# Second chunk of a mixture of experts: third token block first, then two blocks by seven products, gate weights in memory of their own

## The chip, the cores and the metric

The kernel runs on one core of a Trainium2 chip. The metric is the device time of one execution in microseconds (us), lower is better. The core's engines are named as in the profile: PE (TensorE, matmuls; PEld is its weight load), DVE (VectorE), ACT (ScalarE), POOL (GpSimd) and SP, whose queue issues the DMAs. Each engine works through its own instructions in order.

## The reference, cut to what matters

```python
x = attention(q, k, v, n_sink, window)          # (1536, 512) after the heads are put side by side
logits = x @ w_gate                             # 8 experts
P = np.exp(logits - logits.max())
for _ in range(8):                              # rows, then columns
    P /= P.sum(1, keepdims=True) + 1e-09
    P /= P.sum(0, keepdims=True) + 1e-09
    P *= N / E
for e in range(8):                              # w1: 512 x 1024, w2: 1024 x 512
    out += P[:, e:e+1] * (np.maximum(x @ w1[e], 0) @ w2[e])
y = (np.maximum(out @ w_in, 0) ** 2) @ w_out    # 512 -> 2048 -> 512
```

## The kernel before, in words

The work after the attention goes in chunks `c` of 512 hidden columns: 16 of the experts (two per expert) and 4 of the last layer. A chunk has a first layer (x times its part of w1), an evacuation (relu) into `h`, and a second layer (`h` times its part of w2, added to `acc`). The 1536 tokens are three blocks `t` of 512. Every operand of a matmul is kept as a rounded high part and a low part (`xh` and `xl`, `w2h` and `w2l`, `hh` and `hl`), and one product is three matmuls: low times high, high times high, high times low.

A **split** makes the two parts (`pair_split`): ACT copies the raw values into the high part, which rounds them, and POOL subtracts that from the raw values into the low part. Weights come by DMA into one of three buffers of the pool `raw` and are split from there: `units` for w1, `part_w2` for the four pieces of w2. `load_list` is the order of the loads; `next_loads` issues one when an earlier one has been used.

Two forms of the first layer exist. `plain(c, t, f)` computes one 128-column group `f` of one block directly, in 12 matmuls of 512 columns. `fast(c, half, q)` computes, for half of the hidden columns, two blocks together (`q` = 0: blocks 0 and 1) or the two halves of the third block (`q` = 1) by seven products of 6 matmuls each where the direct way takes eight (a scheme of Strassen's kind). It needs four sums of parts of x, T1 to T4, made once by `sums(q)` on DVE, each then split by ACT and POOL, and four sums of parts of w1, made by `unit_sums` on POOL (lines with raw<-raw) and split by `units` with `which` = 3 (tiles s0, s1). T1 is written over the part of `xh` and `xl` that only the direct way needs. The products of a half are p1, p6, p5, p2, p7, p3, p4 in this order, each followed by its evacuation step e1, e6, ... : p2 adds onto the sum in PSUM that p1 began, after ACT has copied it out in e1; likewise p4 after e7, and p3 after e5.

Chunk 0's first layer and most of its second are woven into the attention (`phase_a`; `fill` holds what is left over, finished at the start of `phase_b`). Chunk 1 is all `plain`: block 1, then 0, then 2, while `sums` makes the T tiles between its groups. Chunks 2 to 15 use `fast` for all three blocks. The order of the instructions is written out by hand: within a chunk, `seq` is the list of PE groups, and `put(k, step)` hangs a step behind group `k`. The steps of a group are issued to their engines' queues in the order in which they were put. `GATE_AT` says behind which groups of `phase_b` the next step of `gate` is issued: three steps with 8 matmuls each on the gate's weights `wgz`, one that takes the maximum, and ten that make P. Each of the last eight is a matmul with `ones` of a column sum `cs`, then six small DVE instructions that end in the next `cs`.

The second layer, `second(c, t)`, has four groups of 12 matmuls, each over the four pieces f of `h` and w2 in this order:

```python
for f in (0, 1, 3, 2):
    for x, w in ((hh, wh), (hh, wl), (hl, wh)):
```

## Time and profile before

| | |
|---|---|
| median of 3 runs | 1379.75 us (1378.94 to 1380.15) |
| profiled execution | 1379.64 us |
| its span in the profile | 1377.8 us |
| PE busy | 1363.2 us, 99% of the span |
| POOL busy | 501.3 us, 36% |

The time of an execution includes about 1.8 us around the span that the profile shows. Matmuls overlap in the profile: one of 512 columns lasts 0.39 us there, while the next begins 0.23 us after it, so stages are read from starts and not from the sum of durations. A row of a timeline gives the start and duration in us, then engine, line, operation, out<-in, shape, how many such instructions were merged, and in brackets the idle time before and what ended it.

### The profile page before, as it was taken

What the parts mean: (1) busy time and instruction counts of PE and PEld (TensorE: products, weight loads), DVE (VectorE), ACT (ScalarE), POOL (GpSimd) and SP (SyncE); (2) the same over time, 40 slices, a digit from 0 to 9 for tenths busy, and PEclk for the clock granted to TensorE, in tenths of its full rate; (3) what the DMA queues carried; (4) which work ended last, traced back from release to release, by engine and by line L of the source; (5) the groups of instructions that cost most, each with busy time, mean ns of one, the idle gap of its engine ahead of it and who ended that gap; (6) DMA issues with size and microseconds to landing.
All of it is one profiled execution on the core that took longest, in us unless ns stands there. A gap on an engine that the chain in (4) does not pass through costs nothing.

```text
span 1377.8 us, 18905 instructions
## 1 busy us (share of the span) xinstructions
PE 1363.2 (99%) x7105; PEld 1141.7 (83%) x7105; DVE 955.4 (69%) x1884; ACT 453.1 (33%) x1007; POOL 501.3 (36%) x442
## 2 busy tenths in 40 slices
PE   8999999999999999999999999999999999999998
PEld 5677888888888888888888888888888888888887
DVE  8777369887777777777777768765454568866564
ACT  6776322322232222222232222222232243433331
POOL 4322136524343434424343434423343036543210
PEclk9999999999999999999999999999999999999999
DMA  5222200132313232232313232230102010111101
GB/s 203 81 90 73 78 31 31 62 94 73 124 54 109 79 96 85 92 107 67 118 54 122 70 95 82 92 107 32 61 32 77 16 62 16 62 55 54 46 24 72
DMA packets 61147, 102.53 MB, mean 74 GB/s; under 512 B 3957, under 2 KB 43253, under 8 KB 60789
## 3 DMA queue, kind: packets, MB, share of 16 engines
q1 hardware_dynamic: 61040, 101.22, 23.2%
q8 instruction: 58, 0.95, 0.3%
q14 instruction: 45, 0.36, 0.1%
q10 hardware_dynamic: 4, 0.00, 0.0%
HBM read 89.67 MB, written 11.53 MB: 73 GB/s over the span
## 4 chain that ended last, share of the span: by engine, by line
PE 79%; DVE 1%; ACT 0%; issue 0%; DVEq 0%; ACTq 0%
PE mm L913 42%; PE mm L762 36%; PE mm L930 0%; ACT tx L733 0%; DVE acc L653 0%; DVE tx L734 0%; ACT hh L745 0%; DVE tx L822 0%; DVE hl L746 0%; DVE acc L649 0%; DVE mm L734 0%; DVE raw L578 0%; ACT tx L836 0%; DVE tu L822 0%; DVE raw L565 0%
## 5 line engine op out<-in xcount | busy, mean ns | idle before, releaser
L913 PE MATMUL mm<-w2h,hh 128*128 128x512 f32 (+1 forms) x916 | 357.0, 390 | 0.0
L913 PE MATMUL mm<-w2l,hh 128*128 128x512 f32 (+1 forms) x916 | 355.9, 388 | 0.0
L913 PE MATMUL mm<-w2h,hl 128*128 128x512 f32 (+1 forms) x916 | 355.6, 388 | 0.0
L482 POOL TENSOR_TENSOR w2l<-raw,w2h 128x512 fp32r<-128x512 f32 x76 | 118.5, 1559 | 365.7 <-ACT w2h L481 363.7
L653 DVE SCALAR_TENSOR_TENSOR acc<-mm,P,acc 128x512 f32<-128x512 f32 x168 | 125.7, 748 | 135.6 <-PE mm L913 134.4
L913 PEld LDWEIGHTS mm<-w2h,hl 128*128 128x128 f32 x916 | 172.0, 188 | 35.8
L913 PEld LDWEIGHTS mm<-w2h,hh 128*128 128x128 f32 x916 | 172.1, 188 | 34.6
L913 PEld LDWEIGHTS mm<-w2l,hh 128*128 128x128 f32 x916 | 172.1, 188 | 34.3
L525 POOL TENSOR_TENSOR raw<-raw 128x256 f32<-128x256 f32 x136 | 125.1, 923 | 7.9
L482 POOL TENSOR_TENSOR s0l<-raw,s0h 128x512 fp32r<-128x512 f32 (+1 forms) x36 | 45.5, 1264 | 198.6 <-ACT s0h L481 198.6
L730 ACT ACTIVATE hh<-tx 128x512 fp32r<-128x512 f32 (+1 forms) x112 | 58.8, 525 | 130.0 <-DVE tx L822 129.5
L822 DVE TENSOR_TENSOR tx<-mm,tu 128x512 f32<-128x512 f32 (+1 forms) x136 | 75.6, 556 | 20.9 <-PE mm L762 16.6
L822 DVE TENSOR_TENSOR tx<-mm,tx 128x512 f32<-128x512 f32 (+1 forms) x68 | 37.9, 557 | 57.8 <-PE mm L762 56.5
L740 DVE SCALAR_TENSOR_TENSOR hl<-tx,hh 128x512 fp32r<-128x512 f32 (+1 forms) x112 | 70.1, 626 | 9.7 <-ACT hh L730 9.6
L836 ACT ACTIVATE tx<-mm 128x512 f32<-128x512 f32 x34 | 20.3, 598 | 154.9 <-PE mm L762 153.0
L646 DVE TENSOR_TENSOR acc<-mm,acc 128x512 f32<-128x512 f32 (+1 forms) x49 | 33.2, 677 | 48.2 <-PE mm L913 47.9
L730 ACT ACTIVATE hh<-mm 128x512 fp32r<-128x512 f32 (+1 forms) x68 | 34.0, 501 | 99.2 <-PE mm L762 99.2
L836 ACT ACTIVATE txs<-mm 128x256 f32<-128x256 f32 x34 | 13.0, 381 | 151.3 <-PE mm L762 151.3
L482 POOL TENSOR_TENSOR a0l<-raw,a0h 128x512 fp32r<-128x512 f32 (+1 forms) x38 | 43.0, 1148 | 51.5 <-ACT a0h L481 47.5
L762 PE MATMUL mm<-xl,a1h 128*128 128x512 f32 (+1 forms) x172 | 60.3, 350 | 0.2 <-ACT tx L836 0.2
L762 PE MATMUL mm<-xl,a0h 128*128 128x512 f32 (+1 forms) x172 | 59.8, 348 | 0.0
L762 PE MATMUL mm<-xh,a0h 128*128 128x512 f32 (+1 forms) x172 | 59.8, 347 | 0.0
(262 smaller groups left out, 3149.5 us busy)
## 6 DMA issues: line engine op xcount, KB each, us to landing
raw<-w SPq DMA_DIRECT2D x110, 512.0 KB, 3.7
raw<-win SPq DMA_DIRECT2D x16, 512.0 KB, 4.0
w<-m SPq DMA_DIRECT2D x32, 256.0 KB, 4.6
raw<-wout SPq DMA_DIRECT2D x16, 512.0 KB, 4.0
raw<-qkv SPq DMA_DIRECT2D x8, 624.0 KB, 5.0
raw<-qkv SPq DMA_DIRECT2D x7, 464.0 KB, 3.9
out<-acc SPq DMA_DIRECT2D x11, 256.0 KB, 2.0
wraw<-w SPq DMA_DIRECT2D x2, 1024.0 KB, 6.7
```

Of the source, the lines that this page charges most:

```text
L482: self.nc.gpsimd.tensor_tensor(out=lo, in0=src, in1=hi.bitcast(F32), op=ALU.subtract)
L525: self.nc.gpsimd.tensor_tensor(out=o, in0=x, in1=y, op=op)
L646: nc.vector.tensor_tensor(out=a, in0=ps, in1=a, op=ALU.add)
L653: nc.vector.scalar_tensor_tensor(out=a, in0=ps, scalar=self.P[:, ti, e : e + 1], in1=a, op0=ALU.mult, op1=ALU.add)
L730: nc.scalar.activation(out=hh, in_=src, func=AF.Relu)
L740: nc.vector.scalar_tensor_tensor(out=hl, in0=src, scalar=0.0, in1=hh.bitcast(F32), op0=ALU.max, op1=ALU.subtract,)
L762: self.nc.tensor.matmul(out=ps, lhsT=w[:, kc], rhs=x[:, kc], start=start and k == 0, stop=(k == n - 1), skip_group_check=True,)
L822: nc.vector.tensor_tensor(out=v[name], in0=v[a], in1=v[b], op=ALU.add)
L836: nc.scalar.activation(out=v["s"], in_=v["a"], func=AF.Copy)
L913: self.nc.tensor.matmul(out=ps[:, d], lhsT=x[:, f, s], rhs=w[:, f, d], start=(n == 0), stop=(n == 11),)
```

## The change

The two arrays for the gate get memory of their own (`gw0`), their load and split are issued in the attention at steps 22 and 25, and `ones` is made at the start. The first four steps of the gate are issued behind the groups of `fill`, the others at the places in the second list of `GATE_AT`. Chunk 1 takes block 2 first, by `plain`, with its second layer right behind, then blocks 0 and 1 by `fast` (`mixed`), then their second layers. For this the loads (1, 3, 0) and (1, 3, 1) are added, `unit_sums` and `units` with `which` = 3 for chunk 1, and a form of `sums` that makes T1 first. The four pieces of w2 are put behind groups 0, 0, 1 and 1 in place of 0, 1, 2 and 3.

```diff
--- before.py
+++ after.py
@@ -38,7 +38,10 @@
 NC = NC1 + NC2
 CONV = 3
 CONV_AT = (0, 1, 2, 3, 8, 9, 10, 11, 12, 13, 14, 15)
-GATE_AT = (0, 1, 2, 3, 5, 7, 9, 11, 13, 16, 19, 22, 25, 30)
+GATE_AT = (
+    (0, 1, 2, 3, 5, 7, 9, 11, 13, 16, 19, 22, 25, 30),
+    (12, 14, 16, 18, 20, 22, 25, 28, 31, 36),
+)
 W2_AT = (2, 5, 8, 11)
 NB = 512
 BIG = 1e30
@@ -99,6 +102,8 @@
         )
         self.ident = c.tile([128, 128], F32, name="ident")
         make_identity(nc, self.ident)
+        self.ones = c.tile([128, 128], F32, name="ones")
+        nc.gpsimd.memset(self.ones, 1.0)
         a = self.att
         self.junk = a.tile([128, 1], F32, name="junk")
         self.m0 = a.tile([128, 128], F32, name="m0")
@@ -436,6 +441,9 @@
     def load_list(self, c0):
 
         loads, k = [(c0, which, half) for which in range(2) for half in range(2)], 0
+        if c0:
+            loads[2:2] = [(c0, 3, 0)]
+            loads.append((c0, 3, 1))
         for c in range(c0, NC):
             wide = [(j, 2, 0) for j in range(k, min(k + CONV, 8 * NC2)) if c >= 2]
             k += len(wide)
@@ -668,14 +676,15 @@
         o = 2 * NB * q + w * t
         return tuple(x[:, k : k + 2, o : o + w] for x in (self.xh, self.xl))
 
-    def sums(self, q):
-
-        nc = self.nc
-        T = [
+    def T_tiles(self, q):
+        self.T[q] = [
             self.tp.tile([128, 3, 2, NB >> q], F32R, tag=f"T{q}{t}", name=f"T{q}{t}")
             for t in "hl"
         ]
-        self.T[q] = T
+
+    def sums(self, q, t1_first=False):
+
+        nc = self.nc
 
         def tt(o, a, b, op):
             if isinstance(o, str):
@@ -690,6 +699,30 @@
             hi, lo = self.operand(name, q)
             self.pair_split(hi[:, kc], lo[:, kc], x)
 
+        if t1_first:
+            for kc in range(2):
+                x = tt("x0", f32("B12", 0, kc), f32("B11", 0, kc), ALU.subtract)
+                tt(x, x, f32("B12", 1, kc), ALU.add)
+                tt(x, x, f32("B11", 1, kc), ALU.subtract)
+                put("T1", kc, x)
+            yield
+            self.T_tiles(q)
+            for kc in range(2):
+                t2 = tt("u", f32("B22", 0, kc), f32("B12", 0, kc), ALU.subtract)
+                tt(t2, t2, f32("B22", 1, kc), ALU.add)
+                tt(t2, t2, f32("B12", 1, kc), ALU.subtract)
+                put("T2", kc, t2)
+                yield
+                t4 = tt("x2", f32("B21", 0, kc), t2, ALU.subtract)
+                tt(t4, t4, f32("B21", 1, kc), ALU.add)
+                put("T4", kc, t4)
+                yield
+                t3 = tt("x0", t2, f32("B11", 0, kc), ALU.subtract)
+                tt(t3, t3, f32("B11", 1, kc), ALU.subtract)
+                put("T3", kc, t3)
+                yield
+            return
+        self.T_tiles(q)
         for kc in range(2):
             x = tt("x0", f32("B22", 0, kc), f32("B12", 0, kc), ALU.subtract)
             y = tt("u", f32("B22", 1, kc), f32("B12", 1, kc), ALU.subtract)
@@ -1063,6 +1096,7 @@
                 first = ExitStack()
                 self.wp = self.pool(first, "wp0")
                 self.hp0 = self.pool(first, "hp0")
+                self.gw = self.pool(first, "gw0")
                 with ExitStack() as actx:
                     self.wraw = self.pool(actx, "wraw0")
                     self.att = self.pool(actx, "att")
@@ -1210,6 +1244,7 @@
         self.att_load_v(1)
         for n in (HP - 1, HP):
             self.att_load_qk(n)
+        gw = list(self.gate_weights(self.gw, ("wgz", "wgr")))
         fill = self.filler(gen)
         at = next(fill)
         for u in range(U + 2):
@@ -1272,7 +1307,28 @@
                 self.w_load(0, 1)
             if u == 20:
                 self.general_flag()
+            if u in (22, 25):
+                gw.pop(0)()
         return fill
+
+    def gate_weights(self, pool, tags):
+
+        nc = self.nc
+        self.wgz = pool.tile([128, KD, 128], F32R, tag=tags[0], name="wgz")
+        wgr = pool.tile([128, KD, E], F32, tag=tags[1], name="wgr")
+        hz = self.wgz[:, :, 0:E]
+
+        def load():
+            nc.gpsimd.memset(self.wgz.bitcast(F32), 0.0)
+            nc.sync.dma_start(out=wgr, in_=self.wg)
+
+        def split():
+            nc.scalar.activation(out=hz, in_=wgr, func=AF.Copy)
+            nc.vector.tensor_tensor(
+                out=self.wgz[:, :, E : 2 * E], in0=wgr, in1=hz.bitcast(F32), op=ALU.subtract
+            )
+
+        return load, split
 
     def phase_b(self, c0, first, fill):
 
@@ -1296,27 +1352,29 @@
         ]
         self.loads, self.lk, self.used = self.load_list(c0), 0, set()
         self.next_loads()
-        self.wgz = self.xp_.tile([128, KD, 128], F32R, tag="x0", name="wgz")
-        wgr = self.xp_.tile([128, KD, E], F32, tag="x2", name="wgr")
-        nc.gpsimd.memset(self.wgz.bitcast(F32), 0.0)
-        self.ones = self.xp_.tile([128, 128], F32, tag="x1", name="ones")
-        nc.gpsimd.memset(self.ones, 1.0)
-        nc.sync.dma_start(out=wgr, in_=self.wg)
+        if not c0:
+            for step in self.gate_weights(self.xp_, ("x0", "x2")):
+                step()
         todo = [partial(self.units, c0, half, 0, k) for half in range(2) for k in range(2)]
+        gate, early = self.gate(), 0
         for _ in fill:
             if self.done:
                 self.evac()
                 if todo:
                     todo.pop(0)()
+                if early < 4:
+                    next(gate)
+                    early += 1
         self.evac()
         for step in todo:
             step()
-        hz = self.wgz[:, :, 0:E]
-        nc.scalar.activation(out=hz, in_=wgr, func=AF.Copy)
-        nc.vector.tensor_tensor(
-            out=self.wgz[:, :, E : 2 * E], in0=wgr, in1=hz.bitcast(F32), op=ALU.subtract
-        )
-        gate = self.gate()
+        if c0:
+            for k in range(4 - early):
+                next(gate)
+            t0 = self.sums(0, True)
+            next(t0)
+            for k in range(2):
+                self.unit_sums(c0, 0, k)
         groups = itertools.count()
 
         def run(seq, plan):
@@ -1325,7 +1383,7 @@
                 g()
                 for step in plan.get(k, ()):
                     step()
-                if next(groups) in GATE_AT:
+                if next(groups) in GATE_AT[c0]:
                     next(gate, None)
 
         conv = itertools.chain.from_iterable(self.wide(k) for k in range(8 * NC2))
@@ -1342,23 +1400,36 @@
 
             off = 0
             if not low:
-                run([self.plain(c, 1, 0), *rest], {})
+                run([self.plain(c, 1 + c0, 0), *rest], {})
                 low = first.close() or True
                 self.w2p = self.pool(left, "w2" + n)
                 self.tp = self.pool(left, "T" + n)
                 self.cp, self.T = self.pool(left, "c" + n), {}
-                seq = [self.plain(c, t, f) for t in (1, 0) for f in range(KD)][1:]
+                seq = [self.plain(c, t, f) for t in ((2,) if c0 else (1, 0)) for f in range(KD)]
+                seq = seq[1:]
             elif self.is_fast(c):
                 seq = self.fast(c, 0, 0) + self.fast(c, 1, 0)
             else:
                 seq = [self.plain(c, t, f) for t in (1, 0) for f in range(KD)]
+            mixed = c == c0 == 1
             for k in range(4):
-                put(W2_AT[k] if self.is_fast(c) else k, self.part_w2, c, k)
+                put((0, 0, 1, 1)[k] if mixed else W2_AT[k] if self.is_fast(c) else k,
+                    self.part_w2, c, k)
             if c == NC1:
                 x = [self.x2(2, kc) for kc in range(KD)]
                 seq = sum(([s, *x[k : k + 1]] for k, s in enumerate(seq)), [])
             m = len(seq)
-            if self.is_fast(c):
+            if mixed:
+                m += 18
+                put(2, self.finish)
+                seq += self.second(c, 2) + self.fast(c, 0, 0) + self.fast(c, 1, 0)
+                seq += self.second(c, 1)
+                for half in range(2):
+                    for k in range(2):
+                        if half:
+                            put(1 + k, self.unit_sums, c, half, k)
+                        put((k, 4 + k)[half], self.units, c, half, 3, k)
+            elif self.is_fast(c):
                 (a, b, *e), (f, g, *i) = (self.fast(c, half, 1) for half in range(2))
                 if c < FAST2:
                     seq += self.second(c, 1) + [a, b, f, g]
@@ -1379,16 +1450,19 @@
                     ([s, x[k]] for k, s in enumerate(self.second(c, 0) + self.second(c, 2))), []
                 )
                 wide = lambda k: m + k if k < 8 else m + 2 * k - 8
+            elif mixed:
+                seq += self.second(c, 0)
+                wide = lambda k: m - 8 + k
             else:
                 seq += self.second(c, 0) + self.second(c, 2)
                 wide = lambda k: m + k
             if c in (FAST - 1, FAST2 - 1):
-                t = self.sums(0)
-                for k in range(13):
-                    put(k if c < FAST else min(2 * k, k + 5), next, t, None)
+                t = t0 if mixed else self.sums(0)
+                for k in range(7 if mixed else 13):
+                    put(min(2 * k, k + 5) if c == FAST2 - 1 else k, next, t, None)
                 t = self.sums(1)
                 for k in range(13):
-                    put(m + 8 + k // 2, next, t, None)
+                    put(m + (k // 2 if mixed else 8 + k // 2), next, t, None)
             if c + 1 < NC:
                 if self.is_fast(c + 1):
                     for half in range(2):
```

On POOL, at the first `plain` groups of chunk 1 that follow the last second layer of chunk 0, there stood before (w2l: low part of w2; T0l: low part of T2 to T4; xl: of T1; raw<-raw: sums of w1 parts for chunk 2):

```order
L482 TENSOR_TENSOR w2l<-raw_2016,w2h 128x512 x2
L482 TENSOR_TENSOR T0l<-tx_2293,T0h 128x512
L482 TENSOR_TENSOR w2l<-raw_2049,w2h 128x512 x2
L482 TENSOR_TENSOR T0l<-tx_2344,T0h 128x512
L482 TENSOR_TENSOR xl<-tx_2374,xh 128x512
L482 TENSOR_TENSOR T0l<-tu,T0h 128x512
L482 TENSOR_TENSOR T0l<-tx_2439,T0h 128x512
```

and now, in the same place, with the sums and splits of w1 parts (s0l, s1l) for chunk 1 itself (two more rows follow, one s1l and the last T0l<-tx, of T3):

```order
L490 TENSOR_TENSOR w2l<-raw_2066,w2h 128x512 x2
L490 TENSOR_TENSOR s0l<-raw_2027,s0h 128x512
L490 TENSOR_TENSOR T0l<-tu,T0h 128x512
L490 TENSOR_TENSOR w2l<-raw_2140,w2h 128x512 x2
L490 TENSOR_TENSOR s0l<-raw_2027,s0h 128x512
L533 TENSOR_TENSOR raw_2323<-raw_2323 128x2x128 x2
L490 TENSOR_TENSOR T0l<-tx_2331,T0h 128x512
L533 TENSOR_TENSOR raw_2323<-raw_2323 128x2x128 x2
L490 TENSOR_TENSOR T0l<-tx_2354,T0h 128x512
L490 TENSOR_TENSOR T0l<-tu,T0h 128x512
L490 TENSOR_TENSOR s1l<-raw_2323,s1h 128x512
L490 TENSOR_TENSOR T0l<-tx_2397,T0h 128x512
```

The fourth w2l is the sixth instruction of this piece; it was the fifth before. Behind it stand two T tiles, four sums and two splits of w1 that were further down or were not there.

On PE, the first group of the first second layer of chunk 1 (it is block 2's now, right behind the four `plain` groups of that block; before it was block 1's, with the four groups of block 0 between) reads now, with the engines that each matmul waits for:

```order
L946 MATMUL mm<-w2h,hh 128x512 [waits PE_49,Activation_49]
L946 MATMUL mm<-w2l,hh 128x512 [waits Pool_49]
L946 MATMUL mm<-w2h,hl 128x512 [waits DVE_49]
L946 MATMUL mm<-w2h,hh 128x512 [waits Activation_49]
L946 MATMUL mm<-w2l,hh 128x512 [waits Pool_49]
L946 MATMUL mm<-w2h,hl 128x512 [waits DVE_49]
L946 MATMUL mm<-w2h,hh 128x512 [waits Activation_49]
L946 MATMUL mm<-w2l,hh 128x512 [waits Pool_49]
L946 MATMUL mm<-w2h,hl 128x512 [waits DVE_49]
```

The third wait for POOL, the eighth matmul, is for the fourth piece of w2l (f = 3).

On ACT, behind the second layer of block 2, the last splits of T tiles and the copy e1 of the first `fast` product (L869) stand so now; before, chunk 1 had no such copy:

```order
L489 ACTIVATE T0h<-tu 128x512 [waits DVE_49]
L489 ACTIVATE s1h<-raw_2323 128x512 [waits DMAHW3_49,Pool_49]
L489 ACTIVATE T0h<-tx_2397 128x512 [waits DVE_49]
L489 ACTIVATE s1h<-raw_2323 128x512
L489 ACTIVATE T0h<-tx_2420 128x512 [waits DVE_49]
L869 ACTIVATE tx_2450<-mm 128x512 [waits PE_49,Pool_49]
```

The copy takes the scratch buffer x0 that held the sum for the last T tile, so it waits for POOL to have read that.

## Rows read from the trace of the kernel before

**Rows 1.** The page's part 1: busy time, share of the span, instructions.

```profile
PE 1363.2 (99%) x7105; PEld 1141.7 (83%) x7105; DVE 955.4 (69%) x1884; ACT 453.1 (33%) x1007; POOL 501.3 (36%) x442
```

**Rows 2.** Stretches of the span: length, busy time of the engines, granted TensorE clock.

```profile
core 0: us, PE busy (x) PEld busy (x) DVE busy (x) ACT busy (x) POOL busy (x), PEclk, DMA share, GB/s
0.00:5.00 5.00, 1.01 (x6) 0.99 (x8) 2.23 (x11) 1.49 (x2) 2.11 (x11) 1.00 0.60 184
...
181.70:200.50 18.80, 18.80 (x85) 15.19 (x84) 16.93 (x28) 7.12 (x14) 8.52 (x6) 1.00 0.18 57
200.50:247.35 46.85, 46.63 (x212) 38.43 (x210) 43.50 (x82) 12.14 (x24) 27.57 (x27) 1.00 0.11 34
```

**Rows 3.** Waits of PE over the whole span, longest first.

```profile
PE mm L126 <- DVE nw_f L121: 4.0, 1, 4.0
...
PE mm L762 <- DVE tx L822: 0.6, 1, 0.6
```

**Rows 4.** The chain that ended last: start, length, what.

```profile
288.59 21.79 PE mm L913 x96
310.38 19.04 PE mm L762 x84
```

**Rows 5.** Timeline of PE: starts of the second and third plain group of chunk 1.

```profile
181.70 0.50 PE L762 MATMUL mm<-xl,s0h 128*128 128x512 f32 x1
...
184.59 0.39 PE L762 MATMUL mm<-xl,a1h 128*128 128x512 f32 x1
```

**Rows 6.** Timeline of ACT behind the first of these groups.

```profile
184.79 0.60 ACT L730 ACTIVATE hh<-mm 128x512 fp32r<-128x512 f32 x1 [5.42 <-PE mm L762]
185.29 0.62 ACT L481 ACTIVATE w2h<-raw 128x512 fp32r<-128x512 f32 x1
```

**Rows 7.** Timeline of POOL from there on.

```profile
185.99 1.29 POOL L482 TENSOR_TENSOR w2l<-raw,w2h 128x512 fp32r<-128x512 f32 x1 [23.89 <-ACT w2h L481]
...
189.95 1.74 POOL L482 TENSOR_TENSOR T0l<-tx,T0h 128x512 fp32r<-128x512 f32 x1
191.65 1.73 POOL L482 TENSOR_TENSOR w2l<-raw,w2h 128x512 fp32r<-128x512 f32 x1
194.27 1.30 POOL L482 TENSOR_TENSOR w2l<-raw,w2h 128x512 fp32r<-128x512 f32 x1 [0.89 <-ACT w2h L481]
195.53 1.30 POOL L482 TENSOR_TENSOR T0l<-tx,T0h 128x512 fp32r<-128x512 f32 x1
...
210.06 3.85 POOL L525 TENSOR_TENSOR raw<-raw 128x256 f32<-128x256 f32 x4
```

**Rows 8.** Timeline of DVE in the same microseconds.

```profile
188.75 1.79 DVE L683 TENSOR_TENSOR tx<-xh 128x512 f32<-128x512 f32 x1
190.46 1.78 DVE L683 TENSOR_TENSOR tu<-xl 128x512 f32<-128x512 f32 x1
192.17 0.68 DVE L740 SCALAR_TENSOR_TENSOR hl<-mm,hh 128x512 fp32r<-128x512 f32 x1
```

**Rows 9.** Timeline of DVE: a gate step's first and last, and the instruction behind, twice.

```profile
200.24 0.20 DVE L1005 RECIPROCAL cs<-mm 128x8 f32<-128x8 f32 x1
...
202.76 0.68 DVE L740 SCALAR_TENSOR_TENSOR hl<-mm,hh 128x512 fp32r<-128x512 f32 x1
...
230.17 0.20 DVE L1005 RECIPROCAL cs<-mm 128x8 f32<-128x8 f32 x1
...
231.95 0.67 DVE L646 TENSOR_TENSOR acc<-mm,acc 128x512 f32<-128x512 f32 x1
```

**Rows 10.** The page's part 5: evacuations of the fast products, with mean ns.

```profile
L822 DVE TENSOR_TENSOR tx<-mm,tu 128x512 f32<-128x512 f32 (+1 forms) x136 | 75.6, 556 | 20.9 <-PE mm L762 16.6
...
L740 DVE SCALAR_TENSOR_TENSOR hl<-tx,hh 128x512 fp32r<-128x512 f32 (+1 forms) x112 | 70.1, 626 | 9.7 <-ACT hh L730 9.6
L836 ACT ACTIVATE tx<-mm 128x512 f32<-128x512 f32 x34 | 20.3, 598 | 154.9 <-PE mm L762 153.0
```

**Rows 11.** The page's part 6: loads of weights, KB, us from issue to landing.

```profile
raw<-w SPq DMA_DIRECT2D x110, 512.0 KB, 3.7
```

## The prediction

> **What bounds the kernel now.** I read the page's busy times first, then PE's waits, then stretches around the change, and last the timelines of POOL, ACT and DVE there. PE is busy for 1363.2 of 1377.8 us, POOL for 501.3 [rows 1]. PE's longest wait is 4.0 us at the very start, the rest are below one [rows 3]; in the 18.80 us in which the first T tiles and w2 of chunk 1 are made it does not wait at all, and in the 46.85 us behind them 0.22 us [rows 2]. So a matmul less on PE is worth what it takes, and any new wait of PE is a loss in full. In steady work 96 matmuls of the second layer take 21.79 us and 84 of the first 19.04 us [rows 4], so 0.227 us each: a group of 12 takes 2.72 us, a `fast` product of 6 takes 1.36 us. The look to take is therefore at what PE finds ready when chunk 1 asks for it earlier, or asks for more.
>
> **What is saved.** Chunk 1's first layer had 3 blocks x 4 groups x 12 = 144 matmuls. Now it is 48 for block 2 and 2 x 7 x 6 = 84 for the others: 12 fewer, 2.72 us. The gate's 24 wide matmuls and its small ones are moved, not fewer. PE did not wait where they stood, so moving them saves nothing. The gate's split in the attention adds a small copy on ACT, a small subtraction on DVE, a fill on POOL and one DMA, in the attention, where PE's waits are again those below one us [rows 3]; I take 0.
>
> **First cost: w2 is asked for four groups earlier.** Before, the four groups of block 0 stood between the splits of w2 and the first second layer. Now block 2's second layer comes right behind its own first layer. PE reaches the group plain(1, 2, 1) when it reached the group that begins at 181.70 before (the same matmuls stand ahead of it), and it takes 184.59 - 181.70 = 2.89 us [rows 5]. ACT must evacuate it before it rounds w2: 184.79, then 185.29 [rows 6]; POOL's first w2l begins at 185.99 [rows 7]. This start cannot move, since the order on ACT is the same. Two more groups end at 181.70 + 2.89 + 2 x 2.72 = 190.03, and the eighth matmul of the second layer, which wants the fourth w2l, would issue at 190.03 + 7 x 0.227 = 191.62.
>
> POOL has to finish six subtractions by then. Alone, one follows another after 195.53 - 194.27 = 1.26 us; where DVE has a sum of two arrays in SBUF to make at the same time, after 191.65 - 189.95 = 1.70 us, and such a sum takes 1.78 us in place of some 0.6 us [rows 7, 8]. The evacuation at 192.17, which reads PSUM, keeps its 0.68 us [rows 8]. So the two engines take turns, 0.44 us of POOL's time for each sum of DVE. In this stretch DVE makes T4 and T3 of the first half, two sums each: 185.99 + 6 x 1.26 + 4 x 0.44 = 195.31. PE waits 195.31 - 191.62 = 3.7 us. Without any turn-taking it would be 193.55, and a wait of 1.9 us.
>
> [...]
>
> **Second cost: the T tiles.** Behind the fourth w2l POOL's queue goes on without a pause: a split of s0, four sums of w1 parts, six more T and s1 tiles, then the last, T3. In all 14 subtractions and 4 sums at 3.85 / 4 = 0.96 us [rows 7], with 11 sums of DVE between (T4 2, T3 2, T2 3, T4 2, T3 2): 185.99 + 14 x 1.26 + 4 x 0.96 + 11 x 0.44 = 212.3. The load of (1, 3, 1) does not stop this: its buffer comes free with the second w2l, at about 189, it lands 3.7 us later [rows 11], and its first user is POOL's eighth instruction, after 196. What wants the last T3 first is not the product p7 but e1: its scratch is the one that this T3 was summed in. The copy takes 0.60 us [rows 10], and p2 adds onto the sum that it reads. So p2 can start at 212.9. Without waits PE would be there at 190.03 + 4 x 2.72 + 3 x 1.36 = 205.0. The total of both waits is 7.9 us, 4.2 of it here. At 1.26 us for each subtraction and no turns it is 3.1 us in all. I take the 7.9, because POOL is never idle in the stretch, so each of DVE's sums must take its turn from it.
>
> **Third cost: gate steps two products apart.** Before, the steps from the maximum on stood two or three groups of 2.72 us apart; now six of them stand two products apart, 2.72 us. A full step occupies DVE for 231.95 - 230.17 = 1.78 us, or 202.76 - 200.24 = 2.52 us when POOL is busy [rows 9]. Beside it DVE has the evacuations, 0.56 us for an addition and 0.63 us for the low part of h [rows 10]. From e1's end to the column sum that the fourth of the small `cs` matmuls wants, DVE has 11 such evacuations (6.5 us), the maximum and the exponential's step (about 2.1 us) and three full steps (5.3 us): 13.9 us. PE has nine products there, 12.2 us. That leaves 1.7 us of waits, and 2.2 us more if all three steps are of the long kind. POOL then makes eight sums for chunk 2 (7.7 us), so some are; I take 2.0, with 0 to 4.4 as ends.
>
> **The sum**: -2.7 + 7.9 + 2.0 = +7.2 us on the 1379.64 us of the profiled execution (its span and the 1.8 us around it), which lies 0.1 us below the median of the runs: 1386.9 us.
>
> **The rivals.** A change of 0.2%, 2.76 us, is about what a measurement can tell from none.
> - *The splits keep up, and the saving shows.* 1377.0 us. It decides at six subtractions in 191.62 - 185.99 = 5.6 us, 0.94 us each; no row has one of 512 columns below 1.29 us. Only a later arrival of PE could help, and PE never waits ahead of it. 0.06.
> - *POOL and DVE hardly get in each other's way*, since DVE is held up by its own waits for PE. The waits total 3.1 us and the gate costs 0 to 2.2: 1380.1 to 1382.3 us, no change that can be told. For it, that DVE's later sums hang on evacuations of groups that PE finishes late; against it, the pairs of 1.70 us in a less loaded stretch. 0.18.
> - *DVE becomes the bound in the fast products*: its backlog of sums and the long kind of step, 4.4 in place of 2.0 us: 1389.3 us. 0.10.
> - *PE's clock falls in the two new gaps* (3.7 and 4.2 us). [...] The rows speak against it: in the first 5 us PE was busy for 1.01 and the granted clock read 1.00 [rows 2]. 0.06.
> - *The forecast*, 1384 to 1388.5 us around 1386.9: 0.60.
>
> [...]
>
> **How the numbers follow.** The forecast, DVE's bound and the clock end above 0.2%: 0.76. The second rival and half of the first, which lies on the bound, are no change: 0.20, rounded up with the forecast's own tail; faster 0.04. The range leaves out the first rival and the clock's: 1380 to 1391.5 us.
>
> **What would show it.** In the profile after: PE waiting for POOL's w2l at the first second layer, 2 to 4 us; PE at p2 waiting for ACT's copy e1, and that for POOL's last T3 (T0l), at about 213 us; POOL without idle time from 186 to 212 us; waits of PE for `cs` in the fast products; and 7093 matmuls in place of 7105. Wrong would be: no wait at w2l (then my start of POOL or its 1.26 us is wrong), or waits of PE for a DMA (then the loads, which I call hidden, are late), or a shift of the time at which chunk 1 begins (then the attention pays for the gate's split).

## The result, and where the time went

The changed kernel takes 1389.07 us (median of 6 runs, 1388.15 to 1390.12), the kernel before 1379.99 (6 runs beside it): a ratio of 1.0068 with a 95% interval of 1.0057 to 1.0078. It is slower, by about 9.1 us; 1386.9 was forecast. The profiled execution after took 1388.15 us with a span of 1386.4.

Part 1 of the page after answers to [rows 1]. The 12 matmuls less are there (7093 in place of 7105), yet PE is busy 1.6 us longer.

```profile
PE 1364.8 (98%) x7093; PEld 1141.3 (82%) x7093; DVE 961.6 (69%) x1894; ACT 457.1 (33%) x1013; POOL 514.5 (37%) x454
```

The waits of PE over the whole span, in total, times and longest, answer to [rows 3]:

```profile
PE mm L131 <- DVE nw_f L126: 4.1, 1, 4.1
PE mm L946 <- POOL w2l L490: 3.6, 1, 3.6
PE ptp L344 <- DVE p L331: 3.0, 2, 2.7
PE mm L795 <- ACT tx L869: 1.3, 1, 1.3
...
PE mm L795 <- DVE tx L855: 0.6, 1, 0.6
```

Two of the new waits are those of the forecast: for the fourth w2l, and at p2 for ACT's copy. The third is not: 2.7 us in the attention, for probabilities (p) that DVE makes.

The chain that ended last after the change; [rows 4] began its steady part at 288.59:

```profile
297.89 21.79 PE mm L946 x96
319.68 19.04 PE mm L795 x84
```

So 9.30 us are lost ahead of the steady part, and nothing more behind it: the spans differ by 8.6, so 0.7 us come back there, which was not traced further. Two marks share this out. The first is ACT's evacuation of chunk 1's second plain group, at 184.79 before [rows 6], on the timeline of ACT after at:

```profile
189.04 0.60 ACT L763 ACTIVATE hh<-mm 128x512 fp32r<-128x512 f32 x1 [5.14 <-PE mm L795]
```

Up to there 4.25 us are lost (further profiles, below, put them in the attention and give the same within their scatter). From this mark to the steady part it took 103.80 us before and takes 108.85: 5.05 more, though 2.72 us of matmuls went; 7.77 us of new losses in chunk 1.

**In the attention.** Timelines of DVE, ACT and PE around the wait, one fence each (start, length, what, idle time before and its end):

```profile
79.17 0.68 DVE L652 COPY acc<-mm 128x512 f32<-128x512 f32 x1
82.00 1.18 DVE L1327 TENSOR_TENSOR wgz<-wgr,wgz 128x32 fp32r<-128x32 f32 x1 [2.15 <-ACT wgz L1326]
...
83.49 0.51 DVE L331 TENSOR_SCALAR_CACHE_REDUCE p<-p,st 128x288 f32<-128x288 f32 x1
```

```profile
80.29 0.60 ACT L375 ACTIVATE pT<-ptp 128x512 f32<-128x512 f32 x1 [2.40 <-PE ptp L344]
80.79 1.06 ACT L209 ACTIVATE qkh<-raw 128x640 fp32r<-128x640 f32 x2
81.75 0.22 ACT L1326 ACTIVATE wgz<-wgr 128x32 fp32r<-128x32 f32 x1
```

```profile
81.16 0.34 PE L612 MATMUL mm<-xl,w0h 128*128 128x384 f32 x1
84.16 0.46 PE L344 MATMUL ptp<-ident,p 128*128 128x128 f32 x2 [2.66 <-DVE p L331]
```

ACT's half of the gate's split is 0.22 us long, but stands behind a copy that waits for PE and behind two conversions of q and k. DVE's half, next on DVE from 79.85, waits 2.15 us for it and takes 1.18 itself; behind it on DVE stand the probabilities that PE transposes next, the first of them at 83.49. PE ran out of other groups at 81.50.

**In chunk 1.** POOL's timeline answers to [rows 7]: the first pair of w2l, the second pair, the last T3.

```profile
190.24 3.01 POOL L490 TENSOR_TENSOR w2l<-raw,w2h 128x512 fp32r<-128x512 f32 x2 [2.31 <-ACT w2h L489]
...
196.16 3.38 POOL L490 TENSOR_TENSOR w2l<-raw,w2h 128x512 fp32r<-128x512 f32 x2
...
214.34 1.28 POOL L490 TENSOR_TENSOR T0l<-tx,T0h 128x512 fp32r<-128x512 f32 x1
```

And stretches of the span, as in [rows 2]: each of the two longest waits, and what follows it.

```profile
core 0: us, PE busy (x) PEld busy (x) DVE busy (x) ACT busy (x) POOL busy (x), PEclk, DMA share, GB/s
81.50:84.16 2.66, 0.00 (x1) 0.04 (x1) 2.06 (x7) 1.23 (x7) 2.29 (x2) 1.00 0.00 0
84.16:88.10 3.94, 3.94 (x17) 2.99 (x18) 3.76 (x22) 1.73 (x6) 0.00 (x0) 0.57 0.01 2
...
196.03:199.59 3.56, 0.00 (x0) 0.00 (x0) 2.35 (x2) 0.63 (x1) 3.56 (x4) 1.00 0.04 15
199.59:203.80 4.21, 4.21 (x12) 3.32 (x13) 2.30 (x3) 0.00 (x0) 4.13 (x4) 0.60 0.57 162
203.80:208.00 4.20, 4.20 (x20) 3.49 (x19) 4.13 (x5) 1.24 (x2) 4.12 (x5) 0.99 0.26 91
```

Behind both waits the granted clock falls toward half, to a mean of 0.57 and 0.60 in the two stretches: behind the second, 12 matmuls start in 4.21 us where 20 do in the 4.20 us after. That is most of the busy time PE has too much.

### The profile page after: what moved, and what is told of

It reads as the page before. It is cut to its first block, busy times and chain, and to the rows that moved or that the text cites. A ratio compares the mean times of both kernels' runs of the same rounds, so it can differ in the third digit from the quotient of the medians.

```text
span 1386.4 us, 18917 instructions
## 1 busy us (share of the span) xinstructions
PE 1364.8 (98%) x7093; PEld 1141.3 (82%) x7093; DVE 961.6 (69%) x1894; ACT 457.1 (33%) x1013; POOL 514.5 (37%) x454
## 4 chain that ended last, share of the span: by engine, by line
PE 79%; DVE 0%; issue 0%; DVEq 0%
PE mm L946 42%; PE mm L795 37%; PE mm L963 0%; DVE acc L661 0%; DVE acc L657 0%; DVE raw L586 0%; DVE tx L855 0%; DVE tu L855 0%; DVE raw L573 0%; DVE acc L654 0%; DVE raw L582 0%; DVE raw L578 0%; DVEq L661 0%; DVE m L590 0%; DVEq L855 0%
## 5 line engine op out<-in xcount | busy, mean ns | idle before, releaser
L533 POOL TENSOR_TENSOR raw<-raw 128x256 f32<-128x256 f32 x144 | 130.3, 908 | 10.2 <-DMA raw<-w 1.1
L490 POOL TENSOR_TENSOR s0l<-raw,s0h 128x512 fp32r<-128x512 f32 (+1 forms) x38 | 48.9, 1289 | 211.2 <-ACT s0h L489 200.2
L855 DVE TENSOR_TENSOR tx<-mm,tu 128x512 f32<-128x512 f32 (+1 forms) x140 | 78.4, 560 | 21.2 <-PE mm L795 16.9
L869 ACT ACTIVATE tx<-mm 128x512 f32<-128x512 f32 x36 | 21.6, 599 | 159.2 <-PE mm L795 154.3
L869 ACT ACTIVATE txs<-mm 128x256 f32<-128x256 f32 x34 | 13.0, 382 | 151.3 <-PE mm L795 151.3
L490 POOL TENSOR_TENSOR a1l<-raw,a1h 128x512 fp32r<-128x512 f32 (+1 forms) x38 | 40.4, 1082 | 59.3 <-ACT a1h L489 59.3
L763 ACT ACTIVATE hh<-mm 128x512 fp32r<-128x512 f32 (+1 forms) x62 | 30.6, 493 | 91.3 <-PE mm L795 91.2
L773 DVE SCALAR_TENSOR_TENSOR hl<-tu,hh 128x512 fp32r<-128x512 f32 (+1 forms) x58 | 59.6, 1028 | 1.5
L210 POOL TENSOR_TENSOR qkl<-raw,qkh 128x672 fp32r<-128x672 f32 (+3 forms) x24 | 33.4, 1413 | 72.2 <-ACT qkh L209 64.3
```

Source lines behind the costliest of these rows:

```text
L210: nc.gpsimd.tensor_tensor(out=cut(lo), in0=cut(raw), in1=cut(hi.bitcast(F32)), op=ALU.subtract)
L490: self.nc.gpsimd.tensor_tensor(out=lo, in0=src, in1=hi.bitcast(F32), op=ALU.subtract)
L533: self.nc.gpsimd.tensor_tensor(out=o, in0=x, in1=y, op=op)
L763: nc.scalar.activation(out=hh, in_=src, func=AF.Relu)
L773: nc.vector.scalar_tensor_tensor(out=hl, in0=src, scalar=0.0, in1=hh.bitcast(F32), op0=ALU.max, op1=ALU.subtract,)
L855: nc.vector.tensor_tensor(out=v[name], in0=v[a], in1=v[b], op=ALU.add)
```

## Experiments

All times are medians. "Start" is the evacuation of chunk 1's second plain group and "steady" the begin of the chain's steady part in the profiled execution, from the same two rows as above; the last column is the time between. The ratio is that to the kernel before, run beside each on the same chip (medians of 1379.59 to 1379.99 us); the runs of this table are spread over more than one chip.

| kernel | us | ratio, 95% interval | start | steady | between |
|---|---|---|---|---|---|
| before | 1379.99 | | 184.79 | 288.59 | 103.80 |
| changed | 1389.07 | 1.0068 [1.0057, 1.0078] | 189.04 | 297.89 | 108.85 |
| gate_only | 1384.51 | 1.0035 [1.0021, 1.0048] | 190.02 | 293.86 | 103.84 |
| split_apart | 1385.02 | 1.0039 [1.0025, 1.0053] | 185.24 | 294.10 | 108.86 |
| w2_first | 1392.19 | 1.0089 [1.0075, 1.0103] | 189.43 | 300.44 | 111.01 |
| t3_x1 | 1387.81 | 1.0061 [1.0047, 1.0075] | 190.90 | 299.61 | 108.71 |
| apart_t3x1 | 1384.74 | 1.0031 [1.0019, 1.0043] | 186.01 | 294.77 | 108.76 |
| fewer_sums | 1386.31 | 1.0048 [1.0034, 1.0061] | 189.30 | 295.39 | 106.09 |
| order | 1383.00 | 1.0023 [1.0013, 1.0033] | 184.29 | 290.98 | 106.69 |
| t4_late | 1382.73 | 1.0021 [1.0011, 1.0030] | 185.85 | 292.41 | 106.56 |
| gate_late | 1382.96 | 1.0022 [1.0013, 1.0031] | 185.64 | 292.16 | 106.52 |
| all | 1384.68 | 1.0037 [1.0023, 1.0050] | 185.13 | 293.61 | 108.48 |
| t4_fewer | 1380.32 | 1.0005 [0.9996, 1.0014] | 185.60 | 290.03 | 104.43 |
| after_again | 1388.78 (one run) | | 189.16 | 298.01 | 108.85 |

The start scatters between executions: five profiles of the changed kernel's attention (changed, w2_first, t3_x1, fewer_sums, after_again) have it from 189.04 to 190.90, with a mean of 189.57, and the seven with the split apart from 184.29 to 186.01, mean 185.39. Their difference, 4.2 us, is the steadier figure for the attention. The latest start, t3_x1's, goes with a longer slow stretch: its granted clock from 88 to 90 us is still 0.50, in the changed kernel 1.00.

### One part alone: gate_only

The kernel before, with the gate's weights in memory of their own, `ones` made at the start, and the load and the split called at these two steps of the attention:

```diff
...
+            if u in (22, 25):
+                gw.pop(0)()
...
```

> The kernel before, with only the gate's weights moved: own memory, load, conversion and split inside the attention at the changed kernel's two places; order of the blocks and the gate's steps as before. Theory A: the attention alone lost about 4.2 us in the changed kernel, because VectorE's half of the split is queued ahead of the next probabilities and waits there for ScalarE's half. Then this kernel takes 1379.99 + 4.2 = 1384.2 us (1383.7 to 1384.8), with one wait of PE for p on VectorE of 2.5 to 2.9 us near 82 us and a granted clock near 0.5 for some 3 us behind it. Rival B, my forecast's own term: the split is hidden, and the 4.2 us come from something else of the change that lies ahead of chunk 1; then 1380.0 us (1379.5 to 1380.5).

1384.51 us, 4.9 over the kernel before: theory A. Its waits hold the same 2.7 us for p, and from the start of chunk 1 on it takes the 103.84 us of the kernel before. So my price of nothing for this part was wrong by all that is lost in the attention.

### One part mended: split_apart

The split's two halves become two calls; DVE's comes one step later than ACT's:

```diff
-            if u in (22, 25):
+            if u in (22, 25, 26):
...
```

> The changed kernel, with VectorE's half of the gate's split called one step of the attention later than ScalarE's half. Theory A (VectorE waits in order for ScalarE): ScalarE's half is done when VectorE comes to its own, the 2.15 us wait on VectorE goes, PE's wait of 2.7 us falls to 0.6 us or less, the clock stays at 1.00, and the time falls by 3.5 to 4.3 us, to 1384.8 to 1385.6. Rival C: the price is VectorE's own 1.18 us, or the 16 KB load and its place in SP's queue, not the wait; then PE's wait stays above 1.2 us or moves to another place, and the time is 1387.5 or more.

1385.02 us, 4.05 less than the changed kernel (3.65 if each is taken from the kernel before beside it): theory A again. The load, the fill, ACT's half and DVE's half are all still there; on DVE's timeline its half now waits for nothing:

```profile
81.98 0.69 DVE L652 COPY acc<-mm 128x512 f32<-128x512 f32 x1
82.58 0.77 DVE L1329 TENSOR_TENSOR wgz<-wgr,wgz 128x32 fp32r<-128x32 f32 x1
```

Chunk 1 shows a second thing. PE's waits there are 3.6 for w2l and now 2.9 for ACT's copy, while the clock stayed up behind the first:

```profile
192.23:195.79 3.56, 0.00 (x0) 0.00 (x0) 2.35 (x2) 0.63 (x1) 3.56 (x4) 1.00 0.08 29
195.79:200.00 4.21, 4.21 (x18) 3.49 (x19) 2.71 (x3) 0.00 (x0) 4.13 (x4) 1.00 0.62 183
```

Yet start to steady takes 108.86 us, as in the changed kernel. There PE had lost 1.6 us to the slow clock and waited 1.6 us less for the copy: POOL's last T3 sets the time, and PE comes late or waits. The five runs agree: 1384.55 and 1385.02 us with a mean granted clock of 1.000, and 1384.98, 1385.07 and 1385.74 with 0.996.

### One backlog or two waits: w2_first, t3_x1, apart_t3x1

```diff
-                put((0, 0, 1, 1)[k] if mixed else W2_AT[k] if self.is_fast(c) else k,
+                put(0 if mixed else W2_AT[k] if self.is_fast(c) else k,
```

> The changed kernel, with all four low parts of the second layer's weights ahead of the first unit and the first T2 on POOL (two of them move up by one step; nothing else moves). Theory D (one debt of POOL): POOL works without a break from 190.2 to 222 us, so the order only decides where PE pays. The first wait falls from 3.6 to 1 us or less, the last T3 low still ends near 215.6 us, and the waits behind it grow from 1.3 to 5 to 6 us; the time is 1388.3 to 1389.5, the changed kernel's. Rival E (two separate waits): the first wait goes and the second stays near 1.3 us; then 1384 to 1385.5 us.

The rival is out: the first wait went (0.2 us), and the others grew to 5.0 us. The last T3 ends at 214.57 + 1.26 = 215.83 us where it ended at 215.62. So far theory D; but the time is 1392.19, 2.7 us above its range. The rows of PE's waits and of the windows behind them:

```profile
PE mm L795 <- ACT tx L869: 3.2, 1, 3.2
...
PE mm L795 <- POOL T0l L490: 1.8, 1, 1.8
```

```profile
214.00:216.00 2.00, 0.00 (x0) 0.00 (x0) 0.00 (x0) 0.14 (x1) 2.00 (x3) 0.50 0.01 3
216.00:218.00 2.00, 1.49 (x4) 1.22 (x5) 1.48 (x4) 0.46 (x1) 1.84 (x3) 0.50 0.79 260
218.00:220.00 2.00, 2.00 (x7) 1.24 (x5) 0.18 (x2) 0.53 (x1) 1.84 (x4) 0.50 0.00 0
```

The slow clock, which began behind the earlier of these waits, the one for T0l that ends at 210.05, now outlasts the last T3; nothing of POOL hides it there, and PE pays for it: 2.2 us more between the marks.

```diff
-                t3 = tt("x0", t2, f32("B11", 0, kc), ALU.subtract)
+                t3 = tt("x1", t2, f32("B11", 0, kc), ALU.subtract)
```

> The changed kernel, with T3 built in a scratch tile that no later step of the fast products shares with ScalarE's first copy; every instruction stays at its place. Theory F (the second wait is the shared scratch tile): ScalarE's copy no longer waits for the last T3 low, the second block of p2 starts 1.3 us earlier, T3's product comes some 1.4 us behind it and meets a T3 low that is just done, so 1387.6 to 1388.2 us. Rival G: the wait only moves to T3's own product, since POOL is as late there; then PE waits for T0l on POOL about 1 us and the time stays 1388.6 to 1389.5.

By its median, 1387.81, theory F. But its runs lie in two groups (1387.3 to 1387.8, and two at 1390.2 to 1390.4), and the profiled one is of the upper. In it the wait for the copy is gone and T3's product does not wait, but the clock (0.50 from 201 to 207 us) has taken the gain back: 108.71 us between the marks, where the changed kernel has 108.85. That it is 2.1 us longer than the changed kernel's profiled execution lies ahead of the mark. The lower group has no trace.

> The split_apart run's kernel with T3 in the scratch tile that ScalarE's first copy does not share. Theory D (one backlog of POOL): the wait of 2.9 us for ScalarE's copy goes, but T3's own product, about 1.4 us behind, waits for the last T3 low instead, some 1.2 to 1.6 us; 1383.3 to 1384.0 us. Theory F (the shared tile alone makes the second wait): all 2.9 us go; 1381.8 to 1382.5. If the clock of PE falls behind the first wait, as in the changed kernel's profile, PE arrives 1.7 us later and that wait shrinks by as much, with the same end.

1384.74 us (1382.36 to 1385.38), 0.3 less than split_apart: neither. In the profiled execution, 1385.13, no wait follows the first, since the clock is near half behind it (0.50 from 197 to 201 us), and start to steady takes 108.76 us. Whether T3's product would wait with a full clock no trace shows; the fastest run, 1382.36 us at a mean granted clock of 0.999 in place of the profiled 0.996, lies in theory F's range and below theory D's, but it is one run.

### What sets POOL's pace: fewer_sums

In the changed kernel, without the sums' low terms, which are then missing from the result (two lines of T2, one each of T3 and T4):

```diff
-                tt(t2, t2, f32("B22", 1, kc), ALU.add)
-                tt(t2, t2, f32("B12", 1, kc), ALU.subtract)
...
```

> The changed kernel without eight of VectorE's additions with two inputs in SBUF: T2, T3 and T4 of the third block's partner sums are built from the high parts alone (the low parts' terms are left out of the result); every other instruction stays. Theory I (POOL's pace is set by turns with VectorE, the price I put at 3.1 us quiet and 7.9 with turns): POOL's low parts take 1.28 us in place of 1.75, the fourth w2l ends 1.5 us sooner (first wait 1.9 to 2.2 us), the last T3 low 3 to 4 us sooner, and the second wait goes; 1384.5 to 1386.5 us, with the attention's 4.2 us still in it. Rival J (POOL's own work alone): its lows stay at 1.6 to 1.75 us, the waits stay at 3.6 and 1.3 us, and the time at 1388.5 to 1389.5.

1386.31 us: theory I. Where DVE's sums are gone, POOL's subtractions follow one another as if alone (the changed kernel has 1.78 and 1.75 here):

```profile
205.17 1.30 POOL L490 TENSOR_TENSOR T0l<-tx,T0h 128x512 fp32r<-128x512 f32 x1
206.43 1.29 POOL L490 TENSOR_TENSOR T0l<-tu,T0h 128x512 fp32r<-128x512 f32 x1
```

The last T3 ends 22.7 us after the first w2l began (190.50 to 213.16) in place of 25.4. So the turns with DVE hold 2.7 us of POOL's time, and 2.8 us of the time between the marks. Not all went: 2.7 us for w2l and 1.1 for the copy stayed, more than theory I had; the clock held behind them (1.00 from 196 to 228 us).

### Mending the order: order, t4_late, gate_late, all

The order run has the split apart, the four w2l first, T3 ahead of T4 and in x1, and the second half's weights behind all T:

```diff
-                put((0, 0, 1, 1)[k] if mixed else W2_AT[k] if self.is_fast(c) else k,
+                put(0 if mixed else W2_AT[k] if self.is_fast(c) else k,
...
-                            put(1 + k, self.unit_sums, c, half, k)
-                        put((k, 4 + k)[half], self.units, c, half, 3, k)
+                            put(6, self.unit_sums, c, half, k)
+                        put((k, 11)[half], self.units, c, half, 3, k)
```

> The changed kernel with VectorE's half of the gate's split one step later, as in the split_apart run, and POOL's work ahead of the seven products in the order in which PE asks for it: the four w2l, s0l and T2, then T3 (in a scratch tile of its own), then T4, for one half of the depth after the other; the sums and splits of the second half's weights (s1) come behind all T. Theory D (POOL's backlog, paid where its order makes PE ask too early): at POOL's pace in the split_apart run the w2l end about 0.2 us late, T2 near 203, T3 near 205 and T4 near 207 us, all ahead of their products, and s1l some 1 us late at most; both waits go, and the time falls by 5.5 to 6.5 us to 1378.5 to 1379.8, just under the kernel before. Rival H: POOL is late whatever the order, so PE waits 2 to 4 us for s1l or for the next chunk's sums; then 1381 to 1383.

1383.00 us: 2.0 below split_apart, not 6. POOL is no longer late (it idles 1.3 us ahead of each later T low, for ACT and DVE), and neither theory has the new waits of PE:

```profile
PE mm L1034 <- DVE cs L1028: 2.7, 2, 1.4
PE mm L795 <- ACT tx L869: 1.7, 1, 1.7
```

The copy now stands on ACT behind the conversion of the second T4, which waits for DVE's sums; and the gate's steps, which cost 0.4 us in the changed kernel, cost 2.7.

```diff
-                    put(min(2 * k, k + 5) if c == FAST2 - 1 else k, next, t, None)
+                    put(k + 2 * (mixed and k > 4) if c == FAST - 1 else min(2 * k, k + 5),
+                        next, t, None)
```

> The order run's kernel, with the second T4 two places later, behind ScalarE's first copy of the fast products. Theory K (in the order run ScalarE's copy stands behind the conversion of that T4, which waits for VectorE's sums): the wait of PE for that copy, 1.7 us, goes; T4's low part still ends some 0.5 us before its product; 1.3 to 1.9 us below the order run, 1381.1 to 1381.7 by its median. Rival L: VectorE is as late at the next step, the wait moves on to T4's product or to the gate's sums, and the time stays at 1382.5 to 1383.5.

1382.73 us: rival L. The copy's wait went, and the gate's `nm` (1.0 us) and `cs` (1.8) wait in its place.

```diff
-    (12, 14, 16, 18, 20, 22, 25, 28, 31, 36),
+    (14, 18, 22, 25, 27, 29, 31, 34, 38, 42),
```

> The T4 run's kernel, with the gate's ten late steps spread wider: every fourth group within the seven products, every second within the second layer, the last three in the next chunk's products. Theory M (two gate steps stand too close for VectorE's chain of some 4 us between them): the two waits for cs, 2.7 us in the order run, go; 2.2 to 2.8 us below the T4 run, 1378.3 to 1379.5 by its median, so just under the kernel before (1379.7). Rival N: the steps moved into the next chunk delay VectorE there, and PE waits for its sums; then within 1 us of the T4 run.

1382.96 us: rival N. In the products the steps wait no more; in the second layer, where DVE has the next T sums ahead of them, they wait 2.4 us, and a product waits 1.1 us for a scratch tile that POOL's T4 low holds.

The next run takes these waits one by one (the steps at 14, 18, 22, 24, 29, 33, 36, 39, 42, 45; s1's sums two places and the next chunk's sums four places later).

> The gate_late run's kernel with three moves that its profile asks for: the second T4's low part ahead of POOL's sums for s1 (the product that uses T4's scratch tile next waited 1.1 us for it), the gate's steps out of the second layer, where VectorE's partner sums for the third block stand ahead of them (2.4 us of waits), into the products, and the next chunk's eight sums on POOL four places later, clear of VectorE's work in the products. Theory Q (what is left over the kernel before are these waits of PE, 3.5 us, and nothing else): 1382.96 - 3.5 = 1379.5, from 1378.8 to 1380.3, so about the kernel before (1379.8) or just under. Rival R (VectorE and POOL together are full through the third block's sums and the products, so a wait taken from one place comes up at the next): 1381.5 to 1383.

1384.68 us, worse than even the rival: the places that I made free were paid for elsewhere. s1's conversion on ACT now waits 2.1 us for POOL's later sums with an evacuation behind it, and PE waits as follows (of the third row 0.6 us are in the kernel before too, [rows 3]):

```profile
PE mm L1034 <- DVE cs L1028: 2.1, 3, 1.5
PE mm L795 <- ACT tx L869: 1.5, 1, 1.5
PE mm L795 <- DVE tx L855: 0.9, 2, 0.6
...
PE mm L795 <- POOL s1l L490: 0.6, 1, 0.6
```

### What is left: t4_fewer

The t4_late run's kernel without the same eight additions:

> The t4_late run's kernel without the eight additions that the fewer_sums run left out too (the low parts' terms of T2, T3 and T4 are left out of the result). It asks what holds that kernel 2.9 us above the kernel before although it issues 12 products' matmuls less. Theory R (VectorE's sums of T, slowed by POOL, make VectorE late for the gate's steps and the products' sums): without them the gate's two waits, 1.0 and 1.8 us, go for the most part, and the time falls by 2 to 3.5 us to 1379.2 to 1380.7. Rival S (the gate's chain across PE, VectorE and ScalarE is too long for its two groups of room, whatever VectorE has ahead): the gate's waits stay at 2 us or more, and the time stays within 1.2 us of 1382.7.

1380.32 us, the kernel before's time within 0.2%: the size is theory R's, but the gate's waits do not go. PE still waits 2.7 us for the gate, as rival S says (all for `cs` now). In the two profiles the gain lies in the clock, which fell to 0.50 behind t4_late's gate wait of 1.6 us and stayed up here:

```profile
220.00:222.00 2.00, 1.99 (x5) 0.99 (x3) 1.83 (x7) 0.00 (x0) 1.92 (x3) 0.50 0.07 24
```

```profile
220.00:222.00 2.00, 2.00 (x11) 1.67 (x11) 1.79 (x6) 0.34 (x1) 1.46 (x2) 1.00 0.00 0
```

The first row is t4_late's, the second t4_fewer's: 5 matmuls and 11 in the same 2 us. Yet the runs do not let the clock be the cause of the 2.4 us between the medians. Four of t4_late's ten have a mean granted clock of 1.000, which leaves no room for the profiled fall (a fall of that length takes 0.001 off the mean), and they take 1382.77 to 1383.59 us; the six at 0.998 take 1381.64 to 1383.24. With the clock up that kernel is no faster, so the gain comes with the additions that are gone, as theory R has it. What PE waits for in the runs at 1.000 no trace shows. Even with the sums' price gone the 2.72 us do not show, since PE waits as long for the gate.

### The clock once more: after_again

> The changed kernel once more, for the granted clock behind its two longest waits. Theory O (whether the clock falls behind a wait of 2.7 to 3.6 us differs from one execution to the next): the waits are the same to 0.1 us, while the clock may stay at 1.00 behind one or both. Rival P (the program alone decides): the clock is near 0.5 for some 3.4 us behind both waits again.

1388.78 us, the same waits (3.6, 2.7, 1.3), and the clock near half behind both longer ones again (0.50 from 86 to 88 us, 0.59 from 200 to 204); 108.85 us between the marks. Among all profiles it fell behind the attention's wait in six of six, and behind a w2l wait of 3.6 us in four of five. The one where it did not, split_apart, has up to there the instructions of apart_t3x1, where it did, but with T3 in another scratch tile and on another chip. The runs of split_apart alone, all on one chip, settle it: two of the five have a mean granted clock of 1.000, as the profiled one, and three have 0.996, so their clock fell, though no trace shows behind which wait. An execution decides, not the program alone: theory O in that, although this run by itself looks like rival P.

## Why the forecast came out, and where it failed

The total was near (1386.9 for 1389.07, within the range), but as the sum of errors of both signs, and in that by luck: in the profiles 4.25 us too little for the attention, some 2.1 too much for chunk 1 (7.2 forecast, 5.05 measured), and 0.7 that came back behind it. 1389.07 lies just above the forecast's own 1384 to 1388.5 and, by number, at the rival with DVE as the bound, whose mechanism the changed kernel does not show.

- **What is saved**, 2.72 us: right, 7093 matmuls at 0.227 us each in the steady part. It is more than paid back.
- **The gate's split in the attention, "I take 0"**: this is the step that failed, by 4.25 us in the profile, 4.2 as a mean of profiles, and 3.7 to 4.9 by medians, each against the kernel before beside it. I named PE's short waits as the cover and looked no further. The price is not the split's 0.22 and 1.18 us but its place: DVE's half ahead of the probabilities, ACT's half behind work that waits for PE. The forecast's own test, a shift of the time at which chunk 1 begins, showed it.
- **First cost, 3.7 us**: 3.56 measured. POOL began at 185.99 + 4.25 = 190.24 to the hundredth, and the fourth w2l ended at 199.54 where 195.31 + 4.25 was forecast. The price with turns was the right one: fewer_sums has 1.30 us without DVE's sums where 1.75 stood with them.
- **Second cost**: the place and the mechanism were right (w2_first and t3_x1), the size less so. The last T3 ended at 215.62, 0.9 us earlier than 212.3 + 4.25: POOL's 25.38 us from the first w2l to there hold only about nine of the eleven turns with DVE. Of the 4.2 us forecast PE shows 1.29, because it came late with a slow clock; with a full clock 2.9 (split_apart).
- **Third cost, 2.0 us for the gate's steps**: 0.4. The sum counted it on top of POOL's waits, but while PE waits for POOL, DVE catches up: ahead of the first product's sum at 216.28 it stands idle for 3.7 us. In order, t4_late and t4_fewer, where POOL's waits are gone, 2.7 to 2.8 us come up. The two terms overlap and should not have been added.
- **The rival with the clock**: I let the first 5 us of [rows 2] speak against it, with PE idle and the granted clock at 1.00. That says nothing of a wait in the midst of matmuls. The profile before does show a fall, at its end, where I did not look: behind the last matmul, which ends at 1371.9, the granted clock reads 0.83 from 1374 to 1376 us and 0.50 in the last 1.8 us. The rival's premise came true behind the longer waits; the price of the fall is hidden in chunk 1, where POOL is later still, and stands in the attention's 4.25 us beside the wait of 2.66. The range, up to 1391.5 us, leaves this rival out as if it cost more; no run of the changed kernel shows that: all six have a mean granted clock of 0.994 to 0.997 and take 1388.15 to 1390.12 us. Whether the clock falls differs between executions of one program: of the five runs of split_apart two have a mean granted clock of 1.000 and three 0.996.
- **DVE as the bound in the products**: not in the changed kernel, but this is what the mended ones ran into, as far as t4_fewer shows it.

About 0.9 us of the 7.77 in chunk 1 (3.56 + 1.29 + 0.4 + 1.6 for the clock are 6.85) was not assigned. No run beat the kernel before: with the attention mended and POOL's order mended the change still costs 2.9 to 3.3 us, in waits for DVE and the gate. Whether a layout exists that keeps the 2.72 us stays open; a fourth buffer for raw weights, which would let s1's sums run in POOL's idle time ahead of chunk 1, was not tried.

## What to carry to other kernels

A short operation that two engines share is priced by its place in both queues: list what stands ahead of the half that is waited for, and what stands behind the half that waits. Waits that one late engine causes are a single debt: moving its work about moves the wait (w2_first took 3.6 us down to 0.2 and brought the 1.3 behind it up to 5.0), and other engines' lateness hides beneath it and comes up when it is paid. So before terms are added, ask which of them lie in the same microseconds.

## What the runs showed of the hardware

Behind a wait of PE amid matmuls the granted clock can fall to 0.50, the lowest reading in these profiles, in one execution of a program and not in another (split_apart: a mean of 1.000 in two runs, 0.996 in three). In the profiles it fell behind the attention's 2.7 us in six of six and behind 3.6 us for w2l in four of five; it also fell behind 1.8 us for T0l (w2_first) and 1.6 us for `cs` (t4_late), and did not behind 2.7 us for w2l (fewer_sums) or 2.9 us for the copy (split_apart). It stayed low for about 3.4 us behind the changed kernel's waits of 2.7 and 3.6 us and for about 10 us in w2_first. In the profile before, whose waits of PE are all below one microsecond behind the start, it fell only behind the last matmul.

A 128x512 subtraction of POOL takes 1.28 and 1.29 us while DVE is idle (the changed kernel from 213.09 us), 1.29 and 1.30 where DVE's sums are left out (fewer_sums from 205.17) and 1.75 to 1.78 us beside DVE sums of two SBUF arrays (the changed kernel from 206.23 to 213.14). Such a sum takes 0.68 us while POOL is idle (before, at 197.84) and up to 1.67 us beside POOL (changed, at 206.90).
